# Neighbourhood attention on one core: the first steps reordered, V projected in six matmuls, and the low shift of V in two transfers

## The chip, the cores and the metric

The kernel runs on one core of a Trainium2 chip. The metric is the device time of one execution in microseconds (us); lower is better. The engines are TensorE (PE; its weight loads are shown apart as PEld), VectorE (DVE), ScalarE (ACT), GpSimd (POOL) and SyncE (SP), which here only issues transfers.

## The reference

Each pixel of a 224 x 224 image with 192 channels attends to 7 x 7 neighbours that lie two pixels apart, clipped at the border. Everything is bf16.

```python
H = W = 224; C = 192; ks, dil = 7, 2; half = 6
qkv = x @ wqkv
q, k, v = (qkv[..., :C], qkv[..., C:2*C], qkv[..., 2*C:])
r0 = clip(arange(H) - half, 0, H - 1 - 12)      # first of the 7 rows, the same for columns
...                                             # nidx: the 49 neighbours r0 + 0, 2, .. 12
logits = einsum('bnc,bnkc->bnk', q, k[nidx]) * C ** -0.5
p = softmax(logits)
out = einsum('bnk,bnkc->bnc', p, v[nidx]) @ wo
```

## The kernel before

**Algebra.** Neither Q nor K is made. The setup forms A = wq wk^T (scaled; tiles AW) and W' = wv wo (tiles WP). G = x A is made per query tile, the scores are G against x itself, and V' = x W' already holds the output projection. The 192 channels are split into 128 + 64, so each product has two passes: XA holds the 128, XB the other 64. The partitions that XB has left carry marks: one-hot rows and columns and large negative numbers, which mask keys outside a query's window. G carries the matching marks. `g_col` and `g_row` write these, and `marks` the ones in XB.

**Tiling.** Dilation 2 splits the image by the parity of rows and of columns. `rc` is the row parity. The two column parities `cc` sit side by side in most tiles. There are 14 steps `n` (7 row tiles `ti` by 2 row parities), and each has 7 pairs `m` of column blocks. A column block `s` is 16 rows by 8 columns of queries per parity. `k` counts the 98 pairs.

**Stages of a pair.** `stage1`: the scores into `s` (PE), their maximum `nmx` (DVE). `stage1b`: exp into `p` (ACT). `stage2`: transposes of `p` into `pt_ps` (PE), copied to `pt_sb`. `stage3`: `pt_sb` times V into `o_ps` (PE). `stage4`: division by the sum, and the output transfers. Pair k runs stage 1, pair k - 1 stage 2, and pair k - 2 stages 3 and 4 in the same iteration.

**Work for the next step.** It lies between the pairs. `g_items` makes G in four groups of column blocks: two `whole` products (`pg`, evicted to `g`), and one `halves` product (`pgh`, evicted to `gx`, from which POOL copies into `g`, L456). `v_item` makes one of the 14 V blocks: `v_mms` (L336) issues eight matmuls of 192 columns into `pv`, in two halves h of 64 partitions that lie side by side on PE, and the result is evicted to VF (`vf`). V's lhsT is XS (`xs`): `sort_items` copies a band of 16 image rows from XA and from X1 into the order that V needs, three copies for each row parity. A V block needs two neighbouring bands. `xb_items` copies X1 into XB, two copies. `load_items` issues three transposing loads per band on SP's queue. X1 has two buffers.

**The shifted copies of V.** A query half of 8 rows reads 16 key rows. VD (`vd`) holds V with its halves moved: `vd_low` sends VF[64:128] to VD[0:64] and `vd_high` sends VF[0:64] to VD[64:128]. Both are transfers between SBUF tiles, with 14 blocks of 385 columns in all. `vd_low(rc, 0, 7)` stands at pair m = 5 and 7 to 14 at m = 1 of the next step. VF of that parity is written anew, block by block, from the next step's first pair on. Before the first step VD[0][0:64] is filled by two transfers from VF[1] on ACT's queue (L642); these values only meet probabilities that are zero.

**Order.** `in_order` fixes every engine's program order as it is written in the code, so an engine stands still when its next instruction is not ready. POOL's outputs of block 0 (`out_dram<-o_s`, L588) and its sorts go through the list `pool_q`. Each pair takes four items from it with `pool_do(4)`, and new sorts go to its front. Step 0 is special: bands 0 and 1 are copied and sorted by DVE and POOL before the first pair, and `first_sort` and `v_first` make the upper half of step 1's V. In step 0 the evictions are split between ACT and DVE by the place of an item in a list (L702).

Of the kernel before, what the change touches and what calls it, by code (L numbers as in the profile page):

```python
# [8 lines left out]
BF = mybir.dt.bfloat16  # L9
# [89 lines left out]
def kernel(  # L99
# [212 lines left out]
    for which in range(2):  # L312
        for key in ((0, 0), (1, 0), (0, 1), (1, 1)):
# [4 lines left out]
            if which:  # L318
                nc.scalar.copy(out=WP[key][p0:p0 + cn, :], in_=pt[p0:p0 + cn, 0:C])
# [16 lines left out]
    def v_mms(pv, at):  # L336
        for cc in range(2):
            for pas in range(2):
                for h in range(2):
                    k = 1 if pas else 2 * cc  # L340
                    nc.tensor.matmul(pv[64 * h:64 * h + 64, cc * C:(cc + 1) * C], lhsT=at(k, h), rhs=WP[(cc, pas)][:], start=(pas == 0), stop=(pas == 1))  # L341
# [262 lines left out]
    act, dve, pool = nc.scalar.copy, nc.vector.tensor_copy, nc.gpsimd.tensor_copy  # L604
    pool_q = []
# [23 lines left out]
    sort1 = sort_items(1, 0, pool)  # L629
    for it in sort1[2:] + sort1[:2]:  # L630
        it()
# [10 lines left out]
    for (c0, c1) in ((7, 14), (0, 7)):  # L642
        nc.scalar.dma_start(out=VD[0][0:64, c0:c1, 0:VP - 1], in_=VF[1][0:64, 7:14, 0:VP - 1])
# [3 lines left out]
    for k in range(NP + 2):  # L647
# [3 lines left out]
        if J:  # L651
# [5 lines left out]
            if n == 0:  # L657
                w128 = (v0[:9] + gw0[2:4], v0[9:] + gw0[4:6], gw0[6:8] + vs[0:3], gw[0:2] + vs[3:6], gw[2:4] + vs[6:9], gw[4:6] + vs[9:12], gw[6:8] + vs[12:])[m]
# [6 lines left out]
            if k == 0:  # L665
                marks(1, MM, 2 * MM, dve)
# [21 lines left out]
        first = n == 0 and k >= 2  # L688
        if k >= 2 and not first:
            stage4(pairs[k - 2], 1)  # L690
# [11 lines left out]
        for i, it in enumerate(w128):  # L702
            it(n == 0 and (i in (0, 3 if m == 2 else 4) if first else i % 2 == 1))
            if n == 0 and it is v0[6]:
                vd_high(0, 13, 14)
                vd_high(0, 0, 6)
            if n == 0 and it is v0[13]:
                vd_high(0, 6, 13)
            if first and i == 0:
                stage4(pairs[k - 2], 1)  # L710
            if k == 1 and i == 1:
                xb2.pop(0)()
            if it is vs[6]:
                vd_high(rc1, 0, 7, nc.scalar if n == 0 else nc.sync)
            if it is vs[13]:
                vd_high(rc1, 7, 14, nc.scalar if n == 0 else nc.sync)
        if n == 0 and m == 0:
            xb2.pop(0)()
# [64 lines left out]
```

## Time and profile before

| | us |
|---|---|
| median of 3 runs | 361.81 (361.01 to 361.90) |
| the profiled execution | 360.78 |
| its span | 359.0 |
| PE busy / PEld busy | 332.3 / 306.7 |
| DVE / ACT / POOL busy | 314.3 / 308.5 / 283.0 |
| granted TensorE clock, mean | 0.996 |

The profile shows one execution. Its span runs from the first instruction of the program to the last. The profiled execution took 1.78 us more than its span. Rows of a timeline read: start, duration, engine, line, operation, output tile <- input tiles, shape, count, and in brackets how long the engine had been idle and what ended that. Rows of a window read: length, then busy time and number of instructions of each engine, the granted clock, the share of the DMA engines and GB/s. A wait row gives total, number and longest.

### The profile page before, as it was taken

The numbers are of one execution on the slowest core, as the hardware profiler recorded it, in microseconds if no ns is written. First come the engines' busy times: TensorE is split into PE (matmuls) and PEld (weight loads), VectorE is DVE, ScalarE is ACT, GpSimd is POOL, SyncE is SP. The second block draws the span as 40 slices with busy tenths as digits, with TensorE's granted clock in tenths as the row PEclk, the third lists the DMA queues.
The fourth block names the chain that finished last, engine by engine and source line by source line (L and its number), as shares of the span: only waits on it lengthen the run. The fifth ranks groups of instructions, "written<-read, shape, count | busy, mean of one in ns | idle before, by whom it ended". The sixth has DMA issues, their size and how long they took to land.

```text
span 359.0 us, 19453 instructions
## 1 busy us (share of the span) xinstructions
PE 332.3 (93%) x8120; PEld 306.7 (85%) x8120; DVE 314.3 (88%) x741; ACT 308.5 (86%) x824; POOL 283.0 (79%) x448
## 2 busy tenths in 40 slices
PE   4778997998999999999999999999999999999872
PEld 2666876997999999999989998899999999999762
DVE  8977996997998989889989999799998989989893
ACT  6456776997999999999999998999999989999893
POOL 8976899999896987969869699596995878374182
PEclk9999999999999999999999999999999999999998
DMA  9999986899988989789898998988989855645424
GB/s 188 214 187 171 184 178 163 173 176 189 154 199 193 191 175 176 177 200 201 167 179 188 179 199 187 188 184 181 194 185 188 182 139 125 138 101 116 107 67 91
DMA packets 137539, 60.79 MB, mean 169 GB/s; under 512 B 88578, under 2 KB 136927, under 8 KB 137452
## 3 DMA queue, kind: packets, MB, share of 16 engines
q1 hardware_dynamic: 129124, 55.63, 78.0%
q10 hardware_dynamic: 3048, 2.23, 3.3%
q0 software_dynamic: 5280, 1.71, 2.9%
q8 instruction: 63, 1.03, 1.2%
q14 instruction: 24, 0.20, 0.2%
HBM read 0.29 MB, written 19.27 MB: 54 GB/s over the span
## 4 chain that ended last, share of the span: by engine, by line
PE 71%; POOL 12%; DVE 9%; ACT 4%; issue 2%; DMA 2%; DVEq 0%; ACTq 0%; POOLq 0%
PE s L497 15%; PE pv L341 15%; PE o_ps L536 15%; PE pg L421 10%; PE pt_ps L526 10%; PE pgh L421 5%; POOL out_dram L588 3%; POOL xs L170 3%; ACT p L507 2%; POOL g L456 2%; POOL xb L160 2%; DMA vd<-vf 2%; DVE xb L160 1%; DVE nmx L499 1%; POOL out_dram L565 1%
## 5 line engine op out<-in xcount | busy, mean ns | idle before, releaser
L507 ACT ACTIVATE p<-s,nmx 128x224 bf16<-128x224 f32 x392 | 149.7, 449 | 25.0 <-DVE nmx L499 21.5
L499 DVE TENSOR_REDUCE nmx<-s 128x2 f32<-128x392 f32 (+1 forms) x196 | 102.6, 564 | 19.8 <-PE s L497 18.4
L456 POOL COPY g<-gx 64x512 bf16<-64x512 bf16 (+1 forms) x110 | 62.1, 564 | 52.7 <-ACT gx L331 47.3
L341 PE MATMUL pv<-wp,xs 128*64 128x192 bf16 x1624 | 92.3, 249 | 11.7 <-DVE xs L366 3.6
L341 PEld LDWEIGHTS <-xs 128*64 128x64 bf16 x1624 | 78.7, 111 | 24.3 <-issue 7.6
L559 DVE TENSOR_TENSOR o_sb<-o_ps,rs 128x384 bf16<-128x384 f32 x169 | 94.2, 557 | 5.9
L331 ACT CAST vf<-pv 128x384 bf16<-128x384 f32 x193 | 87.3, 519 | 11.5 <-PE pv L341 9.4
L588 POOL DMA_DIRECT2D out_dram<-o_s x150 | 84.3, 569 | 9.0 <-DVE rs L542 7.8
L497 PE MATMUL s<-xa,g 128*64 128x196 bf16 (+6 forms) x990 | 82.8, 233 | 1.6 <-DVE g L329 0.8
L536 PE MATMUL o_ps<-vd,pt_sb 128*64 128x193 bf16 x784 | 81.8, 246 | 2.4 <-ACT pt_sb L527 2.1
L497 PE MATMUL s<-xb,g 128*64 128x196 bf16 (+7 forms) x990 | 82.3, 232 | 0.6 <-DVE g L329 0.4
L536 PE MATMUL o_ps<-vf,pt_sb 128*64 128x193 bf16 x784 | 81.8, 246 | 0.0
L497 PEld LDWEIGHTS <-g 128*64 128x64 bf16 x1980 | 78.2, 110 | 4.1 <-issue 2.0
L536 PEld LDWEIGHTS <-pt_sb 128*64 128x64 bf16 x1568 | 71.6, 109 | 4.0 <-ACT pt_sb L527 3.2
L527 DVE COPY pt_sb<-pt_ps 128x1024 bf16<-128x1024 bf16 x92 | 63.1, 686 | 5.9 <-PE pt_ps L526 0.8
L526 PE MATMUL pt_ps<-ident,p 128*64 128x128 bf16 x1552 | 63.9, 219 | 0.0
L526 PEld LDWEIGHTS <-p 128*64 128x64 bf16 x1552 | 57.3, 110 | 4.7
L331 ACT CAST g<-pg 128x512 bf16<-128x512 f32 (+4 forms) x136 | 57.5, 468 | 2.4 <-PE pg L421 2.2
L421 PEld LDWEIGHTS <-aw 128*64 128x64 bf16 x1320 | 55.5, 110 | 3.9 <-issue 0.6
L421 PE MATMUL pg<-xb,aw 128*64 128x512 bf16 (+9 forms) x440 | 54.5, 269 | 0.2 <-DVE xb L160 0.2
L421 PE MATMUL pg<-xa,aw 128*64 128x512 bf16 (+9 forms) x440 | 52.8, 270 | 0.1
L170 POOL COPY xs<-xa 128x896 bf16<-128x896 bf16 x52 | 47.4, 939 | 1.4
(73 smaller groups left out, 281.3 us busy)
## 6 DMA issues: line engine op xcount, KB each, us to landing
vd<-vf SPq DMA_DIRECT2D x47, 336.9 KB
out_dram<-o_sb SPq DMA_DIRECT2D x156, 96.0 KB
vd<-vf ACTq DMA_DIRECT2D x4, 336.9 KB
out_dram<-o_s POOLq DMA_DIRECT2D x78, 9.0 KB, 3.7
out_dram<-o_sb SPq DMA_DIRECT2D x13, 78.0 KB
out_dram<-xs SPq DMA_DIRECT2D x13, 78.0 KB
vd<-vf SPq DMA_DIRECT2D x2, 337.8 KB
xa<-in_x_dram SPq DMA_TRANSPOSE x28
```

Source lines behind the costliest of these rows:

```text
L331: nc.scalar.copy(out=out_, in_=in_)
L341: nc.tensor.matmul(pv[64 * h:64 * h + 64, cc * C:(cc + 1) * C], lhsT=at(k, h), rhs=WP[(cc, pas)][:], start=(pas == 0), stop=(pas == 1))
L421: nc.tensor.matmul(o, lhsT=l, rhs=r, start=(pas == 0), stop=(pas == 1))
L456: nc.gpsimd.tensor_copy(out=G[rc][cc][p:p + 64, 1, s0:s0 + ns, :], in_=gx[p:p + 64, 0:ns * 128].rearrange("p (s q) -> p s q", q=128))
L497: nc.tensor.matmul(o, lhsT=w, rhs=r, start=(pas == 0), stop=(pas == 1))
L499: nc.vector.tensor_reduce(out=nmx[:], in_=_win(s_ps, 0, 128, lo, [[256, 2], [16, 14], [1, 16 - lo]]), axis=AX.XY, op=ALU.max, negate=True)
L507: nc.scalar.activation(out=J.p[:, ab, cc, :, z:z + 112].rearrange("p q (r k) -> p q r k", k=8), in_=_win(s_ps, 0, 128, cc * 256, [[8, 2], ...
L526: nc.tensor.transpose(pt_ps[64 * h:64 * h + 64, 4 * ab + 2 * cc + q, :], J.p[:, ab, cc, q, 64 * h:64 * h + 64], ident[:])
L527: (nc.scalar.copy if J.n == NSTEP - 1 and J.m < 5 else nc.vector.tensor_copy)(out=J.pt[:], in_=pt_ps[:])
L536: nc.tensor.matmul(o_ps[64 * h:64 * h + 64, cc * 193:cc * 193 + 193], lhsT=J.pt[:, 4 * ab + 2 * cc + q, 64 * h:64 * h + 64], rhs=V[h][:, ( ...
L559: nc.vector.tensor_tensor(out=o_sb[:], in0=_win(o_ps, 0, 128, 0, [[194, 2], [1, C]]), in1=rs[:].unsqueeze(2).to_broadcast([128, 2, C]), op ...
L588: pool_q.append(lambda dst=dst, p=p, m=n * nj, cc=cc: nc.gpsimd.dma_start(out=dst.rearrange("j i c -> i j c"), in_=o_sb[p:p + m, cc, :]))
```

## The change

1. **V in six matmuls.** The two 64-row passes of W' now lie side by side in one tile WB. `v_mms` issues two matmuls of 384 columns (the 64 leftover channels, for both column parities) and then four of 192, which add to the same accumulators. All 203 V blocks are made so.
2. **The fill of VD[0][0:64]** is one ACT copy of a broadcast column (64 partitions x 14 x 385) after the last W' eviction, and the two transfers on ACT's queue are gone.
3. **Band 1's sort for parity 0** is split: DVE does two of its three copies and the marks of XB[1] (before: in the first pair) ahead of the first V. POOL does the third, and `g_col` for blocks 4 to 13 only after it (before: ahead of all three).
4. **Band 3's** XB copies and sort come at pair 4 of step 0 (before: 5), **band 4's** at pair 3 of step 1 (before: 4).
5. **`vd_low` of blocks 0 to 6** becomes two transfers: 0 to 3 at pair 4 and 4 to 6 at pair 5. This holds for steps 1 to 11, so eleven transfers are added.
6. Step 0's items stand in a written plan, PLAN. Order and engine of each are those that the lists gave before.

```diff
+    WB = pers.tile([128, 2, C], BF, name="wb")
...
-        WP[key] = pers.tile([128, C], BF, name="wp%d%d" % key)
+        WP[key] = pers.tile([128, C], BF, name="wp%d%d" % key)[:] if cn == 128 else WB[:, key[0], :]
...
+    nc.scalar.copy(out=VD[0][0:64, :, 0:VP - 1], in_=E[0:64, 0:1].unsqueeze(2).to_broadcast([64, NSLOT, VP - 1]))
     setup_cm.__exit__(None, None, None)
...
     def v_mms(pv, at):
+        for h in range(2):
+            nc.tensor.matmul(pv[64 * h:64 * h + 64, 0:2 * C], lhsT=at(1, h), rhs=WB[:].rearrange("p t c -> p (t c)"), start=True, stop=False, skip_group_check=True)
         for cc in range(2):
-            for pas in range(2):
-                for h in range(2):
-                    k = 1 if pas else 2 * cc
-                    nc.tensor.matmul(pv[64 * h:64 * h + 64, cc * C:(cc + 1) * C], lhsT=at(k, h), rhs=WP[(cc, pas)][:], start=(pas == 0), stop=(pas == 1))
+            for h in range(2):
+                nc.tensor.matmul(pv[64 * h:64 * h + 64, cc * C:(cc + 1) * C], lhsT=at(2 * cc, h), rhs=WP[(cc, 0)], start=False, stop=True, skip_group_check=True)
...
-    g_col(0, 0, 4, 10, pool)
     for it in load_items(2):
         it()
     for it in first_sort(dve) + xb_items(0, dve) + xb_items(1, dve) + sort_items(0, 0, dve):
         it()
+    srt = sort_items(1, 0, dve)
+    srt[2]()
+    srt[0]()
+    marks(1, MM, 2 * MM, dve)
+    sort_items(1, 0, pool)[1]()
+    g_col(0, 0, 4, 10, pool)
     for j in range(7):
         v_first(j)(False)
...
-    sort1 = sort_items(1, 0, pool)
-    for it in sort1[2:] + sort1[:2]:
-        it()
...
-    for (c0, c1) in ((7, 14), (0, 7)):
-        nc.scalar.dma_start(out=VD[0][0:64, c0:c1, 0:VP - 1], in_=VF[1][0:64, 7:14, 0:VP - 1])
...
-            if k == 0:
-                marks(1, MM, 2 * MM, dve)
...
-        if 0 < n and m == 5 and n + 2 < NSTEP:
-            vd_low(J.rc, 0, 7)
+        if 0 < n and m in (4, 5) and n + 2 < NSTEP:
+            vd_low(J.rc, *((0, 4) if m == 4 else (4, 7)))
...
-            add = {0: sort_items(1, 1, pool), 1: sort_items(2, 1, pool), 3: sort_items(2, 0, pool), 5: xb_items(3, pool) + sort_items(3, 0, pool)}.get(m, [])
+            add = {0: sort_items(1, 1, pool), 1: sort_items(2, 1, pool), 3: sort_items(2, 0, pool), 4: xb_items(3, pool) + sort_items(3, 0, pool)}.get(m, [])
...
-            if m in (2, 4) and n + 3 < NBAND:
+            if m in ((2, 4) if n > 1 else (3,)) and n + 3 < NBAND:
                 srt = sort_items(n + 3, J.rc, pool)
                 one, two = xb_items(n + 3, pool) + srt[2:], srt[:2]
-                add = (two if m == 4 else one) if n > 1 else one + two if m == 4 else []
+                add = (two if m == 4 else one) if n > 1 else one + two
```

More of the change, by code (lines that the diff above doesn't have):

```diff
@@ L604 @@
     act, dve, pool = nc.scalar.copy, nc.vector.tensor_copy, nc.gpsimd.tensor_copy
+    PLAN = (
+        "Va:0 Vd:1 Va:2 Vd:3 Va:4 Vd:5 Va:6 R-:13:14 R-:0:6 Vd:7 Va:8 Gd:2 Ga:3 X-",
+        "Va:9 Vd:10 X- Va:11 Vd:12 Va:13 R-:6:13 Gd:4 Ga:5",
+        "Gd:6 N- Ga:7 Wa:0 Wd:1 Wa:2",
+        "Hd:0 N- Ha:1 Wa:3 Wa:4 Wd:5",
+        "Hd:2 N- Ha:3 Wa:6 Ta:0:7 Wa:7 Wd:8",
+        "Hd:4 N- Ha:5 Wa:9 Wa:10 Wd:11",
+        "Hd:6 N- Ha:7 Wa:12 Wa:13 Ta:7:14",
+    )
     pool_q = []
@@ L657 @@
             if n == 0:
-                w128 = (v0[:9] + gw0[2:4], v0[9:] + gw0[4:6], gw0[6:8] + vs[0:3], gw[0:2] + vs[3:6], gw[2:4] + vs[6:9], gw[4:6] + vs[9:12], gw[6:8] + vs[12:])[m]
                 w64 = (gh0 + gh)[m + 1:m + 2]
@@ L686 @@
             stage2(pairs[k - 1])
-        first = n == 0 and k >= 2
-        if k >= 2 and not first:
+        if k >= 2 and n > 0:
             stage4(pairs[k - 2], 1)
```

26 lines of the change are left out of this document (14 added, 12 removed).

## The prediction

> **What bounds it now.** I read the page, then the stretches, the waits, and the timelines of PE, VectorE (DVE), POOL and ScalarE (ACT) where PE stands still.
>
> ```profile
> span 359.0 us, 19453 instructions
> PE 332.3 (93%) x8120; PEld 306.7 (85%) x8120; DVE 314.3 (88%) x741; ACT 308.5 (86%) x824; POOL 283.0 (79%) x448
> GB/s 188 214 187 171 184 178 163 173 176 189 154 199 193 191 175 176 177 200 201 167 179 188 179 199 187 188 184 181 194 185 188 182 139 125 138 101 116 107 67 91
> 80.00:90.00 10.00, 8.57 (x212) 7.71 (x208) 7.26 (x19) 7.61 (x23) 9.66 (x14) 1.00 0.84 172
> 160.00:200.00 40.00, 39.96 (x1060) 38.24 (x1056) 36.77 (x89) 37.82 (x103) 35.57 (x51) 1.00 0.92 184
> ```
>
> In a stretch row PE, PEld, DVE, ACT and POOL follow the length. From 160 to 200 us PE is busy all but 0.04 us and ACT rests 2.18 us in 40. There only PE's own work counts. Around 80 to 90 POOL is the fullest engine and PE stands still for 1.4 us. Those stops are the first place to gain:
>
> ```profile
> PE pv L341 <- POOL xs L170: 3.6, 3, 2.3
> ACT vf L331 <- DMA vd<-vf: 1.3, 1, 1.3
> 60.31 0.69 PE L341 MATMUL pv<-wp,xs 128*64 128x192 bf16 x12 [2.34 <-POOL xs L170]
> 83.93 0.36 PE L341 MATMUL pv<-wp,xs 128*64 128x192 bf16 x4 [0.69 <-POOL xs L170]
> 84.80 0.44 PE L341 MATMUL pv<-wp,xs 128*64 128x192 bf16 x6 [0.52 <-POOL xs L170]
> 225.06 0.52 PE L341 MATMUL pv<-wp,xs 128*64 128x192 bf16 x8 [1.08 <-ACT g L331]
> ```
>
> PE waits 2.34 us for POOL's sort of band 3, 0.69 + 0.52 us for band 4, and 1.08 us behind an ACT that had waited 1.3 us for a low shift still reading the buffer it was to overwrite. Since PE is full afterwards, what goes from these stops goes from the end.
>
> **Part 1, before the first pair.** The chain here is DVE's.
>
> ```profile
> 11.61 5.24 DVE L160 COPY xb<-x 64x1792 bf16<-64x1792 bf16 x4
> 16.88 2.04 DVE L170 COPY xs<-xa 128x896 bf16<-128x896 bf16 x2
> 18.84 0.42 DVE L170 COPY xs<-x 128x896 bf16<-128x896 bf16 x1
> 19.19 0.60 DVE L329 CAST g<-pg 128x24 bf16<-128x24 f32 x4
> 20.80 1.07 DVE L499 TENSOR_REDUCE nmx<-s 128x2 f32<-128x420 f32 x2 [0.35 <-PE s L497]
> 21.79 1.07 DVE L233 COPY xb<-xb 64x3584 bf16<-64x3584 bf16 x1
> 28.47 0.62 DVE L160 COPY xb<-x 64x1792 bf16<-64x1792 bf16 x1 [0.68 <-DMA x<-in_x_dram]
> 11.98 3.12 POOL L256 COPY g<-ch 32x1280 bf16<-32x1280 bf16 x2
> 15.16 1.20 POOL L170 COPY xs<-x 128x896 bf16<-128x896 bf16 x1
> 16.32 2.36 POOL L170 COPY xs<-xa 128x896 bf16<-128x896 bf16 x2
> ```
>
> The same xb copy takes 0.62 us at 28.47, with POOL idle, and 5.24 / 4 = 1.31 us while POOL copies; xs takes 0.42 against 2.04 / 2 = 1.02. Starts and ends interleave: each engine waits for the other's copy to end. After the change POOL's next copy is the last sort of band 1, which needs that band's last load. Six loads of 128 x 1792 x 2 B, 2.75 MB, at the 188 to 214 GB/s of the first two slices from about 2 us on give 16 us (the old row bounds it: the second copy at 16.32 had begun by 17.7). Until then POOL rests, and DVE runs alone: from 11.61, four xb at 0.62, five xs at 0.42 (two are new) and the marks at 1.07 are 5.65 us, ending at 17.3. Before, it got to its first eviction at 19.19, with the marks still to come at 21.79. PE's product is ready by about then:
>
> ```profile
> 7.89 0.31 ACT L319 CAST wp<-prA 64x192 bf16<-64x192 f32 x1
> 12.47 0.48 ACT L331 CAST vf<-pv 128x384 bf16<-128x384 f32 x1 [4.27 <-PE pv L341]
> 17.38 0.56 ACT L331 CAST g<-pg 128x24 bf16<-128x24 f32 x4 [1.25 <-PE pg L421]
> L331 ACT CAST gx<-pgh 128x128 bf16<-128x128 f32 x25 | 5.5, 274 | 0.4 <-PE pgh L421 0.2
> L527 ACT COPY pt_sb<-pt_ps 128x1024 bf16<-128x1024 bf16 x5 | 5.1, 1018 | 0.1
> ```
>
> ACT evicts the first product at 17.38, so DVE's start moves from 19.19 to about 17.4: 1.8 us. The marks' 1.07 us no longer stand behind the first maximum, but ACT follows that maximum, so I add none (bound above 2.5). Below: if the last load comes a little later than DVE or earlier, POOL's three copies (0.93 as later rows have it, twice 3.12 / 2 = 1.56) come between DVE's last ones. DVE then reaches the eviction 0.6 us late and gets back the marks: 0.3 us. I take 1.8: DVE's last sort ends at 16.2, its marks need only start before the load has landed, and the 16 us counts bytes alone. If the load is first by a little, POOL's one sort goes ahead and the gain is about 0.9, between the two.
>
> The new ACT copy has 14 x 385 = 5390 elements. Between the last two rows an element costs (1018 - 274) / 896 = 0.83 ns, so 4.6 us; by 1018 / 1024 it is 5.4. It starts at 8.20 and ends at 12.8 to 13.6, in an idle time of 4.27 us that ended at 12.47. The seven evictions behind it, 0.48 us each, then end by 16.2 to 17.0, still ahead of 17.4: nothing. Without that cover it would cost its 4.6 us. It waits for nothing but POOL's fills of that buffer, which stand ahead of all POOL copies above. The two transfers it replaces, 2 x 64 x 7 x 770 B = 0.69 MB, free 3.5 us of the DMA queues at 0.2 MB/us; DVE's 0.68 us wait at 28.47 should go, but PE's scores were not ready earlier: nothing (to +0.6, within the bound above).
>
> **Part 2, bands 3 and 4.**
>
> ```profile
> 48.09 2.30 POOL L588 DMA_DIRECT2D out_dram<-o_s  x4
> 52.27 3.39 POOL L160 COPY xb<-x 64x1792 bf16<-64x1792 bf16 x2
> 55.72 1.80 POOL L170 COPY xs<-xa 128x896 bf16<-128x896 bf16 x2
> 59.32 0.93 POOL L170 COPY xs<-x 128x896 bf16<-128x896 bf16 x1
> 72.74 4.52 POOL L588 DMA_DIRECT2D out_dram<-o_s  x8
> 78.62 3.39 POOL L160 COPY xb<-x 64x1792 bf16<-64x1792 bf16 x2
> 82.95 1.80 POOL L170 COPY xs<-xa 128x896 bf16<-128x896 bf16 x2
> ```
>
> Each pair lets POOL take four queued items. Band 3's five copies now start where the four output transfers stood: 48.09 + 3.39 + 1.80 = 53.3, then 1.8 us for the next pair's own POOL work (the gap 57.5 to 59.32), then 0.93: done at 56.1 instead of 60.25. PE wanted it at 60.31 - 2.34 = 57.97, so that stop goes, with 1.9 us to spare. The copies for the next step that follow come 3.39 + 1.80 - 2.30 = 2.9 us later, and the four output transfers a pair later; what reads those copies is in the next step.
>
> Band 4's copies now start after the first four of the eight transfers at 72.74: 75.0 + 3.39 + two sorts 1.8 + the next pair's copies 1.3 + 0.9 = 82.4, not 84.75. But POOL has no idle time here and gets no faster from PE's 2.34 us. PE would arrive 2.34 us earlier and wait about 1.5 us, more than now. Across both places the end comes at 82.4 instead of 84.8: **2.3 us** in all, not 3.55. Bounds: 3.55 if POOL keeps up, 1.0 if the moved work makes a later copy late.
>
> **Part 3, the low shift.** Blocks 0 to 3 leave one pair earlier and are smaller, and ACT overwrites block 0 first; the 1.08 us stop at 225 goes. It occurs once in thirteen steps, so it is a near miss that other executions may not have: **1.1**, bounds 0 and 1.3. Eleven more transfers are issued, one per step; their price is below. In SyncE's queue the new one stands behind the output transfers of the pair that reads the blocks last, so its wait has ended when its turn comes and holds nothing up.
>
> **Part 4, six matmuls per V block instead of eight** (also in the diff).
>
> ```profile
> 285.06 0.61 PE L526 MATMUL pt_ps<-ident,p 128*64 128x128 bf16 x15
> 285.45 0.40 PE L421 MATMUL pg<-xa,aw 128*64 128x416 bf16 x2
> 285.64 0.40 PE L421 MATMUL pg<-xb,aw 128*64 128x416 bf16 x2
> 285.97 0.82 PE L341 MATMUL pv<-wp,xs 128*64 128x192 bf16 x15
> 286.58 0.21 PE L497 MATMUL s<-xa,g 128*64 128x98 bf16 x1
> ```
>
> From start to start one matmul takes 0.39 / 15 = 26 ns at 128 columns, 0.61 / 15 = 41 at 192 and 0.19 / 2 = 95 at 416: 0.20, 0.21 and 0.23 ns a column. Two matmuls of 384 columns replace four of 192: 2 x 81 to 88 ns against 164. Over the 154 blocks made while PE is full (11 steps x 14) that is -0.3 to +1.8 us. I take **0**: the new rhs is read contiguously, as in the 128 and 192 rows, and the 416 one in 13 pieces.
>
> **Sum.** 1.8 + 2.3 + 1.1 + 0 = 5.2 us. The profiled execution took 360.78 us (its span 359.0 and 1.78 around it), so 355.6; the median of the runs is 361.81, 1.03 above it, so **356.6 us**.
>
> **Rivals.**
> *The start gives nothing* (0.2): POOL's copies fall between DVE's last three, as above. For it: the load's 16 us and DVE's 16.2 for its last sort lie close. Part 1 gives 0.3: 358.1 us. The Trainium skill (SBUF — State Buffer, "SBUF: two separate sides") says that whichever of the two starts first keeps the shared port for the whole instruction; the 1.31 against 0.62 us agree.
>
> *Everything comes* (0.12): POOL keeps up, the marks' time counts: 2.5 + 3.55 + 1.3 = 7.35, so 354.5 us.
>
> *The weight loader is PE's pace* (0.03): the page's 306.7 us for 8120 loads are 38 ns each; two fewer in 154 blocks are 11.6 us, just within ACT's rest of 2.18 in 40 us: 345 us. Against it: 26 ns at 128 columns is below 38. The Trainium skill (TensorE: Matmul & The Clock Gate, "Back-to-back issue gap") gives about 81 ns at 128 columns and 131 at 512 for a stream of load and matmul; interpolated to 89 at 192 and 114 at 384, that is an estimate of 129 ns saved per block, or 10 us with two matmuls side by side. The trace does not agree: 26 and 41 ns.
>
> *SyncE's queue becomes the pace, slower* (0.06):
>
> ```profile
> 216.89 0.62 SPq L352 DMA_DIRECT2D vd<-vf  x1
> SPq L565 <- DVE o_sb L559: 54.5, 70, 2.4
> ```
>
> Each extra issue takes 0.62 us, 11 x 0.62 = 6.8 us, ahead of output and input transfers in the same queue. It decides once the queue has under 0.62 us of rest per step. Then part 3 is lost and 6.8 - 4.1 = 2.7 us come on top: 364.5 us. Against it: the queue waits 54.5 us on one producer alone, 4 us per step. The Trainium skill (DMA: Bandwidth & Descriptors, "Rules for kernel authors") says to coalesce small transfers into large ones. Its fixed 2.0 us per transfer (same page, "Anatomy of one DMA") would make an estimate of 22 us; no run so far shows that price.
>
> *The stops only move* (0.07): ACT, with 2.18 us of rest in 40, is the true pace, and each stop that PE loses comes back as a wait for an eviction, so only about 0.3 us is left: 361.5 us. Against it: from 80 to 90 ACT is busy 7.61 of 10.
>
> **Chances.** The forecast has 0.52. A measurement of this kernel tells 0.3%, 1.1 us, from no change. Faster: forecast, start, everything, weight loader, 0.87; same 0.07; slower 0.06. The range 354.0 to 360.0 holds the forecast, the start and everything (0.84), with part 4's cost of up to 1.8 on the forecast; the weight loader's 345, SyncE's 364.5 and the stops' 361.5 lie outside.
>
> **What would show it.** Right: the first nmx near 19 us; no POOL wait near 58; a wait of about 1.5 us near 79; no DMA wait of ACT; POOL idle from 12 to 16. Wrong: xb copies still at 1.3 us, the ACT copy over 6 us, pv over 0.35 us a block, or output transfers of SyncE that no longer wait for DVE.

## The result and the profile after

| | before | after |
|---|---|---|
| median of the runs, us | 361.47 (359.65 to 368.30, 21 runs) | 358.71 (356.64 to 362.73, 21 runs) |
| ratio | | 0.9936, 95% interval 0.991 to 0.9961 |
| profiled execution, us | 360.78 | 360.73 |

The changed kernel is 0.64% faster: 2.3 us, between 1.4 and 3.3, where 5.2 were forecast. (Medians are of all runs; ratios and stage times leave disturbed ones out.) The profiled execution of it lies 2.0 us above its median and shows nothing of the gain at its end. So the trace was read by stages: for each pair the start of its first nmx, after against before. These differences are -0.77 us at pair 0, -0.44 at pair 1, -2.50 at pair 8, -2.78 at pair 15, then -1.35 at pair 28, -0.89 at pair 42, +1.38 at pair 56, +0.22 at pair 58 and 0 at the end. Something was gained by 83 us and lost again between 100 and 215 us.

The page of the changed kernel, its span and its busy times:

```profile
span 359.0 us, 18669 instructions
PE 333.0 (93%) x7714; PEld 302.1 (84%) x7714; DVE 312.5 (87%) x743; ACT 312.1 (87%) x825; POOL 280.2 (78%) x446
```

The stretches of the changed kernel (length, then PE, PEld, DVE, ACT, POOL, clock, DMA share, GB/s):

```profile
80.00:90.00 10.00, 8.97 (x196) 7.90 (x193) 8.07 (x20) 8.41 (x26) 9.64 (x16) 1.00 0.92 165
160.00:200.00 40.00, 39.29 (x980) 36.60 (x976) 35.67 (x86) 36.46 (x100) 34.55 (x49) 1.00 0.95 183
```

Around 80 PE now stands for 1.03 us instead of 1.43. But from 160 to 200, where it stood for 0.04, it stands for 0.71. The waits of the changed kernel say for what (total, number, longest):

```profile
PE pv L340 <- DVE xs L368: 4.0, 1, 4.0
PE pv L340 <- ACT gx L333: 3.0, 4, 1.5
DVE o_sb L561 <- DMA out_dram<-o_sb: 2.3, 2, 1.3
PE o_ps L538 <- DMA vd<-vf: 2.1, 3, 1.1
PE pv L343 <- POOL xs L170: 1.0, 1, 1.0
ACT vf L333 <- DMA vd<-vf: 0.7, 2, 0.4
```

The 4.0 us are the wait for the first sorted copy at the start (3.6 before). Of POOL's sorts (3.6 us before) 1.0 is left. In its place PE waits three times for a shifted copy of V, a wait that the list of before does not have. It also waits 3.0 us behind evictions of ACT (0.4 for `gx` before); 1.48 us of them stand at 30.48, 0.32 at 58.05 and 0.64 at 212.48, shortly after ACT itself had stood for 1.82 us (210.78). The timeline of PE in the changed kernel shows where:

```profile
58.05 0.35 PE L340 MATMUL pv<-wb,xs 128*64 128x384 bf16 x2 [0.32 <-ACT gx L333]
82.11 0.27 PE L343 MATMUL pv<-wp,xs 128*64 128x192 bf16 x1 [0.99 <-POOL xs L170]
110.55 0.24 PE L538 MATMUL o_ps<-vd,pt_sb 128*64 128x193 bf16 x1 [1.13 <-DMA vd<-vf]
179.97 0.24 PE L538 MATMUL o_ps<-vd,pt_sb 128*64 128x193 bf16 x1 [0.66 <-DMA vd<-vf]
285.94 0.36 PE L340 MATMUL pv<-wb,xs 128*64 128x384 bf16 x2
286.11 0.36 PE L343 MATMUL pv<-wp,xs 128*64 128x192 bf16 x4
286.27 0.36 PE L340 MATMUL pv<-wb,xs 128*64 128x384 bf16 x2
```

The stop near 58 is down from 2.34 to 0.32 us, the one for band 4 is 0.99 at 82.11, and no stop stands near 225. In the full stage two matmuls of 384 columns take 0.17 us from start to start, as four of 192 do (285.94, 286.11, 286.27).

DVE in the changed kernel, at the start:

```profile
11.61 2.72 DVE L160 COPY xb<-x 64x1792 bf16<-64x1792 bf16 x4
15.87 1.08 DVE L233 COPY xb<-xb 64x3584 bf16<-64x3584 bf16 x1
18.40 0.62 DVE L331 CAST g<-pg 128x24 bf16<-128x24 f32 x4 [1.45 <-PE pg L423]
20.03 1.07 DVE L501 TENSOR_REDUCE nmx<-s 128x2 f32<-128x420 f32 x2 [0.35 <-PE s L499]
26.21 2.43 DVE L160 COPY xb<-x 64x1792 bf16<-64x1792 bf16 x1
28.57 1.05 DVE L501 TENSOR_REDUCE nmx<-s 128x2 f32<-128x420 f32 x2
```

POOL and ACT in the changed kernel:

```profile
16.23 1.51 POOL L170 COPY xs<-xa 128x896 bf16<-128x896 bf16 x1 [4.31 <-DMA xa<-in_x_dram]
25.48 1.80 POOL L170 COPY xs<-xa 128x896 bf16<-128x896 bf16 x2
27.23 0.93 POOL L170 COPY xs<-x 128x896 bf16<-128x896 bf16 x1
54.74 0.93 POOL L170 COPY xs<-x 128x896 bf16<-128x896 bf16 x1
8.23 4.68 ACT L323 COPY vd<-e 64x5390 bf16<-64x5390 bf16 x1
17.95 0.56 ACT L333 CAST g<-pg 128x24 bf16<-128x24 f32 x4 [0.96 <-PE pg L423]
```

DVE's copies run nearly as forecast: 0.68 us each (0.62 forecast) beside an idle POOL, marks done at 16.95. Then DVE waits 1.45 us for PE. And at 26.21 the XB copy of band 2, whose load now lands before DVE asks for it, runs into POOL's three sorts (25.48 to 28.16). It takes 2.43 us, where it took 0.62 before, and the second nmx stands right behind it: 28.57 against 29.01. POOL for its part works without a rest from 16.23, when band 1's load has landed, to 28.16.

### The profile page after: what moved, and what is told of

Same layout as the page of the kernel before. It is cut to its first block, busy times and chain, and to the rows that moved or that the text cites. A ratio compares the mean times of both kernels' runs of the same rounds, so it can differ in the third digit from the quotient of the medians.

```text
span 359.0 us, 18669 instructions
## 1 busy us (share of the span) xinstructions
PE 333.0 (93%) x7714; PEld 302.1 (84%) x7714; DVE 312.5 (87%) x743; ACT 312.1 (87%) x825; POOL 280.2 (78%) x446
## 4 chain that ended last, share of the span: by engine, by line
PE 67%; ACT 9%; DVE 9%; POOL 5%; DMA 5%; issue 3%; DVEq 0%; ACTq 0%; SPq 0%; POOLq 0%
PE s L499 14%; PE o_ps L538 14%; PE pg L423 9%; PE pt_ps L528 9%; PE pv L340 8%; PE pv L343 7%; ACT p L509 6%; PE pgh L423 5%; DMA vd<-vf 4%; DVE nmx L501 2%; POOL xs L170 2%; ACT gx L333 1%; POOL out_dram L590 1%; DMA out_dram<-o_sb 1%; POOL xb L160 1%
## 5 line engine op out<-in xcount | busy, mean ns | idle before, releaser
L501 DVE TENSOR_REDUCE nmx<-s 128x2 f32<-128x392 f32 (+1 forms) x196 | 102.5, 564 | 16.2 <-PE s L499 15.0
L333 ACT CAST vf<-pv 128x384 bf16<-128x384 f32 x193 | 88.8, 526 | 8.5 <-PE pv L343 3.0
L499 PE MATMUL s<-xa,g 128*64 128x196 bf16 (+7 forms) x990 | 82.1, 233 | 1.2 <-ACT p L509 0.3
L340 PE MATMUL pv<-wb,xs 128*64 128x384 bf16 x406 | 72.7, 334 | 9.0 <-DVE xs L368 4.0
L343 PE MATMUL pv<-wp,xs 128*64 128x192 bf16 x812 | 73.2, 250 | 1.0 <-POOL xs L170 1.0
L343 PEld LDWEIGHTS <-xs 128*64 128x64 bf16 x812 | 60.1, 112 | 9.6 <-POOL xs L170 1.2
L423 PEld LDWEIGHTS <-aw 128*64 128x64 bf16 x1320 | 54.6, 110 | 3.2
```

The source lines that it names most:

```text
L333: nc.scalar.copy(out=out_, in_=in_)
L340: nc.tensor.matmul(pv[64 * h:64 * h + 64, 0:2 * C], lhsT=at(1, h), rhs=WB[:].rearrange("p t c -> p (t c)"), start=True, stop=False, skip_g ...
L423: nc.tensor.matmul(o, lhsT=l, rhs=r, start=(pas == 0), stop=(pas == 1))
L499: nc.tensor.matmul(o, lhsT=w, rhs=r, start=(pas == 0), stop=(pas == 1))
L501: nc.vector.tensor_reduce(out=nmx[:], in_=_win(s_ps, 0, 128, lo, [[256, 2], [16, 14], [1, 16 - lo]]), axis=AX.XY, op=ALU.max, negate=True)
```

## The experiments

Three questions were open. Why did part 1 bring 0.45 us instead of 1.8? What makes V's shifted copies late: the number of issues in SyncE's queue, or the transfer engines that carry them? And does each part do alone what it does in the whole? Medians are compared as ratios to the kernel before. The stages come from one profiled execution of each kernel, here for those that the argument needs:

| kernel, times in us | first nmx | second nmx | pair 15 | pairs 15 to 56 | pairs 56 to 93 |
|---|---|---|---|---|---|
| before | 20.80 | 29.01 | 85.98 | 132.43 | 120.01 |
| before, part 1 alone | 19.63 | 28.56 | 85.48 | 132.43 | 119.76 |
| before, part 3 alone | 20.81 | 29.13 | 86.05 | 132.47 | 120.03 |
| before, part 4 alone | 20.81 | 29.29 | 86.60 | 132.68 | 118.66 |
| after | 20.03 | 28.57 | 83.20 | 136.58 | 118.59 |
| after, a second profile | 19.89 | 28.56 | 83.17 | 137.92 | 118.56 |
| after, one low transfer | 19.32 | 28.55 | 84.73 | 135.54 | 119.45 |
| after, low shift in four | 19.87 | 28.67 | 83.30 | 142.11 | 124.25 |
| after, low shift on ACT's queue | 19.57 | 28.56 | 86.91 | 132.27 | 118.56 |
| the same from step 2 on | 19.99 | 28.56 | 83.19 | 134.21 | 119.31 |
| after, on POOL's queue from step 2 on | 20.56 | 28.57 | 84.80 | 132.89 | 118.57 |
| after, band 2's copy late | 19.83 | 27.02 | 81.88 | 134.22 | 118.59 |
| the same, second profile | 19.01 | 26.19 | 81.06 | 133.13 | 118.58 |
| the same, POOL's queue | 20.36 | 27.55 | 82.39 | 132.57 | 118.58 |

Four of these profiles hold a stretch of 3.41 us in which the granted clock was half: part 1 alone from 60.4 us on, one low transfer from 32.4, low shift on ACT's queue from 80.7 and low shift in four from 234.9. The last section says what it costs.

### The changed kernel again, and its parts alone

The changed kernel without an edit:

> The changed kernel once more, beside the others of this group, with a second profile. Theory A (SyncE's queue: its rest per step fell from about 3.2 us to 1.7 us with the eleven added transfers, so late shifts of V stop PE): the PE stops on vd between 100 and 215 us, 2.1 us in the first profile, come again in some of the steps, and SyncE rests under 2 us per step. Theory B (chance: such stops hit either kernel anywhere): they may be missing altogether, with SyncE's rest still under 2 us. Time: 2 to 3 us under the kernel before by both.

Measured: 359.99 us, ratio 0.9942 (0.9906 to 0.9979). The gains at the front come again to 0.03 us (second nmx 28.56, pair 15 at 83.17). The loss from pair 15 to 56 is 5.5 us this time against 4.15: it is of the kernel, but its size changes from execution to execution.

Part 1 alone: the ACT copy in place of the two fill transfers, and the following lines, in place of those that the change takes out:

```diff
+    srt = sort_items(1, 0, dve)
+    srt[2]()
+    srt[0]()
+    marks(1, MM, 2 * MM, dve)
+    sort_items(1, 0, pool)[1]()
     g_col(0, 0, 4, 10, pool)
```

> The kernel before with part 1 alone: the fill of VD by ACT, band 1's sort split between DVE and POOL ahead of the first V, the marks ahead of the first pair. V stays in eight matmuls, so the first V block starts with the copies that are sorted first. If the matmul order of part 4 is what held the first V back, then the first nmx comes at 18.9 to 19.3 us, against 20.80 before and 20.03 with all parts. If it is the XS copies' own times or the weight loads, it comes at about 20.0 here too. In either case the gain at the second pair is below 1 us, for the XB copy of band 2 meets POOL's sorts here as well; at the end 0 to 1 us are left, 360.5 to 361.5.

Measured: 361.11 us, ratio 1.0007 (0.9977 to 1.0037). The first nmx came at 19.63, the second at 28.56, to 0.01 us where the whole change has it. Two rows tell the rest, the first of DVE, the second of PE, in this kernel:

```profile
25.82 2.82 DVE L160 COPY xb<-x 64x1792 bf16<-64x1792 bf16 x1
59.85 0.84 PE L342 MATMUL pv<-wp,xs 128*64 128x192 bf16 x13 [2.34 <-POOL xs L170]
```

The copy ends with POOL's sorts here too, and near 60 PE waits for POOL's sort of band 3 as before. At pair 8 this kernel is 0.02 us ahead of the one before: what the start gives, POOL takes back 30 us later.

Part 2 alone (the edits to bands 3 and 4 of the diff):

> The kernel before with only bands 3 and 4 one pair earlier. The prediction's part 2: PE's stop of 2.34 us near 58 goes and one of about 1.5 us stays near 81: 2.3 us less at the start of step 2. Theory A: SyncE's rest shrinks from then on and 1 to 2 us of it are lost by step 8, so 0.5 to 1.5 us are left at the end; theory B: all 2.3 us are left on the average.

Measured: 360.55 us, ratio 0.9994 (0.9964 to 1.0024). By the interval at most 1.3 us of the 2.3 reach the end when the part stands alone. Where the rest goes is not shown.

Part 3 alone (the two transfers of the diff):

> The kernel before with only the low shift split. Prediction's part 3: 1.1 us faster than the kernel before (0 to 1.3). Theory A: SyncE's rest falls from about 3.2 to 1.7 us per step and PE stops on vd appear: 0 to 2 us slower than the kernel before.

Measured: 361.56 us, ratio 1.0003 (0.9971 to 1.0036). Behind a later PE eleven more issues cost nothing (132.47 against 132.43). The stop at 224 is gone, but 1.3 us are lost at pair 61, near 234.

Part 4 alone (the new `v_mms`, with WB):

> The kernel before with part 4 alone, V in six matmuls instead of eight, the 384-column pair first. Forecast of the prediction: 0, bounds -0.3 to +1.8 us of cost over 154 blocks. [...] If the last-sorted copy, which now goes first, holds blocks back in step 0, 0.3 to 0.9 us more. If the weight loads set PE's pace, over 5 us less.

Measured: 360.85 us, ratio 0.9989 (0.9961 to 1.0017): nothing, as forecast. This kernel has the low shift in one transfer, and pairs 56 to 93 take 118.66: here the stop at 224 is absent without any split, as it is with part 1 alone.

### What makes V's copies late

The low shift in one transfer again, at pair 5, in the changed kernel:

```diff
-        if 0 < n and m in (4, 5) and n + 2 < NSTEP:
-            vd_low(J.rc, *((0, 4) if m == 4 else (4, 7)))
+        if 0 < n and m == 5 and n + 2 < NSTEP:
+            vd_low(J.rc, 0, 7)
```

> The changed kernel with the low shift of blocks 0 to 6 as one transfer at pair 5 again. Theory A: SyncE's rest per step goes back to about 3 us, the stops of PE on vd go, ACT may stop once for about 1 us as in the kernel before: 0 to 2 us faster than the changed kernel. Theory B and the prediction's part 3: about 1.1 us slower than the changed kernel, by ACT's stops on the low shift.

Measured: 360.23 us, ratio 0.9971 (0.9946 to 0.9995). Pairs 15 to 56 still lose 3.1 us, now through ACT, which waits 3.7 us there for transfers to have read VF. (Its later pair 15 comes in part from the half clock at 32.4.) So the split is not the cause of the loss. Its own worth, 0.9971 against 0.9936 and 0.9942, is about 1 us inside the changed kernel, and the intervals overlap: it is not shown.

The other way, four transfers with the same bytes (blocks 0-1, 2-3 at pair 4, 4-5, 6 at pair 5), 22 more issues:

> The changed kernel with the low shift of blocks 0 to 6 in four transfers (2, 2, 2 and 1 blocks) instead of two: same bytes, 22 more issues on SyncE's queue, 1.24 us per step. Theory A: SyncE's rest of 1.7 us per step is used up and PE, ACT or DVE stop more in steps 2 to 10: 2 to 8 us slower than the changed kernel. Theory B (stops by chance): within 1 us of it.

Measured: 372.12 us, ratio 1.0327 (1.0277 to 1.0377): 13.4 us over the changed kernel, 0.61 us for each added issue. That this meets the 0.62 us of one issue so closely is partly chance: four executions were measured, and the profiled one has the stretch at half clock.

Both parts issued from ACT's queue:

```diff
-            vd_low(J.rc, *((0, 4) if m == 4 else (4, 7)))
+            vd_low(J.rc, *((0, 4) if m == 4 else (4, 7)), nc.scalar)
```

> The changed kernel with the two parts of the low shift (blocks 0 to 3 and 4 to 6) issued on ACT's queue instead of SyncE's, in steps 1 to 11. The bytes and the number of transfers stay. Theory A: SyncE's rest rises to 3.5 us or more per step and the stops on vd go: 1 to 2 us faster than the changed kernel, less what 22 issues of 0.6 us cost on ACT where they are not hidden. If instead the transfer engines' throughput is the limit (theory C), the stops on vd stay: same time or slower.

Measured: 362.02 us, ratio 0.9985 (0.995 to 1.0021). All of the loss stands in step 1, at pair 14; ACT's row there:

```profile
78.88 0.58 ACT L333 CAST g<-pg 128x512 bf16<-128x512 f32 x1 [4.62 <-DMA xa<-in_x_dram]
```

The issue stands in ACT's own order, and what ACT has to do behind it waits 4.62 us. The stretch at half clock follows, from 80.7 on. From pair 15 on nothing is lost: 132.27. Hence the same from step 2 on, with step 1 left on SyncE's queue, and then POOL's queue in ACT's place:

> The changed kernel with the two parts of the low shift issued on ACT's queue in steps 2 to 11 and on SyncE's in step 1. With all of them on ACT, one 4.6 us stop of ACT stood in step 1, before an issue that waited for an earlier load, and no stop on vd stood in steps 2 to 10. Theory A (SyncE's queue is the pace in steps 2 to 8): without that stop the gain of 2.4 to 2.8 us that stands at the start of step 2 stays to the end: 356 to 358 us in the profile, 0.990 to 0.993 of the kernel before or better. Theory C (the transfer engines' throughput): the gain shrinks over steps 2 to 8 as it does in the changed kernel.

> The same two parts issued on POOL's queue in steps 2 to 11. Theory A: the stops on vd and on outputs go as on ACT's queue, and POOL, which has about 4 us of rest per step from step 3 on, pays 0.6 us or more per issue: 0.990 to 0.994. Theory C: no gain over the changed kernel. Against both: POOL is full in step 2, where its sorts would come late and stop PE by about 1 us.

Measured: 359.74 us, ratio 0.9967 (0.9935 to 1.0), and 358.69 us, ratio 0.9936 (0.9906 to 0.9965). The stretch from 100 to 200 us of the kernel before, of the changed kernel, of the one with four transfers and of the one on POOL's queue, one row each:

```profile
100.00:200.00 100.00, 99.92 (x2579) 94.94 (x2575) 91.22 (x219) 93.98 (x255) 84.00 (x119) 1.00 0.93 186
```

```profile
100.00:200.00 100.00, 97.79 (x2394) 91.09 (x2390) 88.38 (x211) 90.72 (x247) 82.53 (x118) 1.00 0.93 182
```

```profile
100.00:200.00 100.00, 94.94 (x2305) 88.80 (x2303) 86.20 (x205) 88.41 (x238) 78.58 (x110) 1.00 0.84 175
```

```profile
100.00:200.00 100.00, 99.91 (x2460) 93.82 (x2457) 91.30 (x219) 93.97 (x255) 89.39 (x128) 1.00 0.89 187
```

PE stands for 0.08, 2.21, 5.06 and 0.09 us of the 100. With four transfers the transfer engines are emptier (share 0.84 and 175 GB/s against 0.93 and 182) and PE waits longer. With the same transfers on another queue they move more (187) and PE does not wait. So it is not the engines, but SyncE's order.

Between 86 and 264 us SyncE has 155 issues before and 163 after. An issue that waits for nothing begins 0.05 to 0.1 us after the end of the one before, so only a later start is rest. Before the change 31 issues begin over 0.11 us after the one before, with 14.7 us between them in sum. In the changed kernel it is 4 issues and 1.1 us, or 0.14 us per step of 22.4. Two rows of before, then five of the changed kernel:

```profile
102.67 0.62 SPq L352 DMA_DIRECT2D vd<-vf  x1
103.68 1.10 SPq L565 DMA_DIRECT2D out_dram<-o_sb  x1
```

```profile
101.19 0.62 SPq L354 DMA_DIRECT2D vd<-vf  x1
101.90 1.21 SPq L567 DMA_DIRECT2D out_dram<-o_sb  x2
103.21 0.62 SPq L354 DMA_DIRECT2D vd<-vf  x1
103.92 1.23 SPq L567 DMA_DIRECT2D out_dram<-o_sb  x2
105.24 1.79 SPq L357 DMA_DIRECT2D vd<-vf  x1
```

Before, 0.39 us lie free ahead of 103.68; after, each row begins 0.1 us or less behind the last.

The same rest is 24.9 us (41 issues) with the issues on POOL's queue, and 2.4 us (8 of 154) in the kernel with one low transfer: there the queue is full without any added issue. The time in the issues themselves rises from 149.9 us before to 161.6 after and 162.7 with one low transfer. Eight added issues explain 5.0 of the 11.7 us after; why issues of the same kinds take longer is open, and so whether SyncE is held by the issuing itself or by transfers that still stand in its queue.

Counted over pairs 15 to 56 alone, the kernels of the table with under 2 us of rest lose 1.8 to 9.7 us there against the one before. Those with 7.5 us or more stay within 0.5 us of it, but for one: with the issues on ACT's queue from step 2 on, ACT again waits behind an issue, 2.13 us at 100.69. The second profile of the late copy lies between, with 5.1 us of rest and 0.7 us lost.

But the end says that the move is no gain: the kernel on POOL's queue has the ratio of the changed kernel. Its profile reaches pair 15 later (84.80 against 83.20), but up to there the two programs are the same, so this is chance: DVE waits 2.6 us for a free output tile and PE 1.82 us behind ACT. From pair 15 on it keeps what the changed kernel loses. Why its median is then no lower is open.

### What holds the start back

Two edits to the changed kernel: the four matmuls of 192 columns first in `v_mms`, the pair of 384, whose sorted copy comes last, at the end; and the XB copy of band 2 one pair later:

```diff
-        "Va:0 Vd:1 Va:2 Vd:3 Va:4 Vd:5 Va:6 R-:13:14 R-:0:6 Vd:7 Va:8 Gd:2 Ga:3 X-",
-        "Va:9 Vd:10 X- Va:11 Vd:12 Va:13 R-:6:13 Gd:4 Ga:5",
+        "Va:0 Vd:1 Va:2 Vd:3 Va:4 Vd:5 Va:6 R-:13:14 R-:0:6 Vd:7 Va:8 Gd:2 Ga:3",
+        "Va:9 Vd:10 X- Va:11 Vd:12 X- Va:13 R-:6:13 Gd:4 Ga:5",
```

> The changed kernel with two edits to its start: in v_mms the four 192-column matmuls go first and the 384-column pair, which needs the copy XS that is sorted last, goes last; and the XB copy of band 2 moves from pair 0 to pair 1. Theory of part 1: the forecast 1.8 us shrank to 0.45 because the first V blocks now wait for the last of the sorted copies, and because DVE's XB copy of band 2 ran against three POOL copies (2.43 us instead of 0.62). Then the first nmx comes at about 19.1 us (20.03 in the changed kernel, 20.80 before), and by the second pair the kernel is 1.5 to 2.0 us ahead of the one before (0.44 in the changed kernel). Rival on part 1: PE's slow pace of the first blocks (0.64 us each) comes from something else, not from the order; then the first nmx stays at 20.0 and only the collision's part, up to 1.8 us, comes at the second pair or not at all. On the end: if SyncE's queue is the pace of steps 2 to 8, whatever is gained here is given back, and the time stays within 0.4 us of the changed kernel's (358.7); if PE is the pace throughout, 357.0 to 357.5.

Measured: 356.88 us, ratio 0.9872 (0.9835 to 0.9909). First nmx 19.88, second 27.06. The queue did not take the gain back: the theory said 358.7 +/- 0.4. In this kernel, and in the next, the start flag stands on the first matmuls of both column parities, and V does not hold the full product; the instructions are the same in number and shape as in the later kernels, which set the flag on the first parity's alone.

With the low shift on POOL's queue from step 2 on as well:

> The kernel of the front edits, with both parts of the low shift issued from POOL's queue from step 2 on and from SyncE's in step 1. The bytes and the number of transfers are those of the changed kernel. If the issues on SyncE's queue are what gives the gain back, then what the front edits gain lasts: 1.0 to 1.7 us below the same kernel without the front edits (358.7 there), 357.0 to 357.7, a ratio to the kernel before of about 0.989 to 0.991, and no stop of PE for vd after 90 us of over 0.3 us. If the transfer engines themselves are the limit, it comes out at 358.5 to 359, as the changed kernel does.

Measured: 356.37 us, ratio 0.9848 (0.9816 to 0.988).

Then each edit alone. The order of the matmuls:

```diff
-        for h in range(2):
-            nc.tensor.matmul(pv[64 * h:64 * h + 64, 0:2 * C], lhsT=at(1, h), rhs=WB[:].rearrange("p t c -> p (t c)"), start=True, stop=False, ...)
...
-                nc.tensor.matmul(pv[...], lhsT=at(2 * cc, h), rhs=WP[(cc, 0)], start=False, stop=True, ...)
+                nc.tensor.matmul(pv[...], lhsT=at(2 * cc, h), rhs=WP[(cc, 0)], start=(cc == 0), stop=False, ...)
+        for h in range(2):
+            nc.tensor.matmul(pv[64 * h:64 * h + 64, 0:2 * C], lhsT=at(1, h), rhs=WB[:].rearrange("p t c -> p (t c)"), start=False, stop=True, ...)
```

> The changed kernel with the order of the six matmuls turned in all V blocks: the four of 192 columns first, the pair of 384 last. The accumulators of both column parities are started by the first matmul alone. If the two front edits act through the second pair's nmx, this one alone does little: the first nmx comes 0 to 0.8 us earlier (19.2 to 20.0), by the moment at which PE's half pace ends, the second stays 0.45 us ahead of the kernel before, and the time is that of the changed kernel, 358.3 to 359.1. Rival: the order counts in every step (the weights of the 192-column matmuls load under the 384-column pair or not), then the end is 1 to 2 us below the changed kernel's without an earlier second pair.

Measured: 359.20 us, ratio 0.9938 (0.9912 to 0.9963): nothing. The first nmx came at 19.30, the second at 28.56 all the same. And the copy of band 2 alone:

> The changed kernel with the XB copy of band 2 at pair 1 instead of pair 0, nothing else. If the collision of DVE's copy with POOL's three sorts is what kept part 1 at 0.45 us, the second nmx comes 1.3 to 2.0 us ahead of the kernel before, though the first does not come earlier than 20.0. At the end: 357.0 to 357.6 if the gain lasts; 358.3 to 359.1 if SyncE's queue takes it back.

Measured: 356.01 us, ratio 0.9849 (0.9832 to 0.9867): all of it. DVE in this kernel:

```profile
19.83 1.07 DVE L501 TENSOR_REDUCE nmx<-s 128x2 f32<-128x420 f32 x2 [0.35 <-PE s L499]
27.02 1.07 DVE L501 TENSOR_REDUCE nmx<-s 128x2 f32<-128x420 f32 x2 [0.92 <-PE s L499]
29.32 0.73 DVE L160 COPY xb<-x 64x1792 bf16<-64x1792 bf16 x1
```

The copy takes 0.73 us at 29.32, behind POOL's sorts, and the second nmx waits for PE alone. With the start changed and the copy in its old place the second nmx came between 28.55 and 28.57 in eight profiles of nine (28.67 in the ninth), whether the first stood at 19.30 or at 20.56; with the copy late it follows the first by 7.17 to 7.19 us in seven profiles. The old place was a wall at the end of POOL's sorts, 28.16 us, that nothing tried ahead of it moved.

Both edits, accumulators started once, and the same on POOL's queue:

> Both front edits, with the accumulators of both column parities started by the first matmul alone; instructions and order are those of the first kernel with both edits. The same time, 356.4 to 357.4, a ratio to the kernel before of 0.984 to 0.991. If that gain came from the matmul order and the copy in equal parts, the two single edits give half each; if from the copy alone, the copy alone gives all of it.

> Both front edits and the low shift on POOL's queue from step 2 on, the accumulators started once. As the same kernel before it, 355.9 to 357.0. If the issues on SyncE's queue still cost when the start is earlier, 0.5 to 1.5 us below the kernel with the front edits alone; if not, the same within 0.4 us.

Measured: 357.24 us, ratio 0.9901 (0.9865 to 0.9937), and 356.70 us, ratio 0.9877 (0.9858 to 0.9897). The order of the matmuls adds nothing to the copy. Last, the late copy with SyncE's queue and with POOL's, side by side:

> The changed kernel with the XB copy of band 2 at pair 1, as before, beside the next kernel. Again 355.7 to 356.5 us, a ratio of 0.983 to 0.988; the second nmx 1.3 to 2.0 us ahead of the kernel before, and the stops for vd in steps 2 to 8 between nothing and 2.5 us in sum.

> The same, with the low shift on POOL's queue from step 2 on. Theory: a SyncE queue with 1 to 2 us of rest per step makes vd late in some executions and not in others, by up to 4 us; taking 22 issues from it removes these stops, so its executions lie closer together and the median is 0.3 to 1.0 us lower, 355.0 to 355.9, with no stop for vd after step 2. Rival: the stops came from the start's lateness alone, and with the later copy the queue costs nothing; then both kernels agree within 0.3 us, and POOL's extra issues may even cost 0.2 to 0.5 us.

Measured: 355.94 us (355.13 to 358.73), ratio 0.9869 (0.9825 to 0.9914), and 357.08 us (355.97 to 357.66), ratio 0.9872 (0.984 to 0.9905). POOL's queue again takes the stops away (pairs 15 to 56 in 132.57 us), its six executions lie closer together, and again the median gains nothing. So the best version found is the changed kernel with band 2's XB copy one pair later, 356.0 us, about 5 us below the kernel before.

## Why the prediction was partly wrong

The sign, the parts 2 and 4 and the range held; the size did not. That the range held is partly luck: it was drawn for a start that gives little, not for a gain of part 2 that is lost again behind pair 15.

**Part 1 (1.8 us, measured 0.45).** The copies, the ACT fill (4.68 us for 4.6) and POOL's rest to 16.2 came as written. "PE's product is ready by about then" did not hold in the profiled execution: PE ran at half pace until 16.8 us instead of 14.6 (the last section), so that ACT evicts G at 17.95, not 17.38, and DVE starts at 18.40, not at 17.4. That is chance: where the half pace ended at 14.66, the first nmx came at 19.01, as forecast. The first V block starts at 11.74 instead of 10.84, since it now begins with the copy sorted last, but this costs under 0.1 us: with the half pace ending at 14.67 and 14.66 the seven blocks were through by 15.39 with the four of 192 columns first and by 15.47 with the pair of 384 first. The step that failed was another: "DVE's 0.68 us wait at 28.47 should go, but PE's scores were not ready earlier: nothing". The load that lands earlier lets DVE start its copy 2.3 us earlier, among POOL's sorts, and the copy grows by 1.8 us. Moving only that copy brought the second nmx to 27.02 and 26.19, 2.0 and 2.8 us ahead of before. The prediction had the price of that collision in its own rows, 1.31 against 0.62, and did not carry it to the next place where the two engines meet.

**Part 2 (2.3 us, measured 2.3).** From pair 1 to pair 15 the difference grows from 0.44 to 2.78. Three of four profiles of the same program up to there show these 2.3 us; the fourth shows 0.7 and has the two waits that were named with POOL's queue. Band 3's copies were done at 55.67 (forecast 56.1). The stop for band 4 became 0.99 us, not 1.5, and so the end there comes at 82.11, not 82.4. Alone the part shows no such gain at the end; why is open.

**Part 3 (1.1 us, a size not settled).** The stop at 224 is gone, but it goes in the kernels with part 1 alone and with six matmuls alone too, and moves in the one with the split alone. It was the near miss that the prediction called it.

**Part 4 (0, measured 0).** 0.17 us for two matmuls of 384 columns and for four of 192. The rival in which the weight loader is PE's pace is out: PEld fell from 306.7 to 302.1 us and the pairs kept their time.

**SyncE's queue (0.06, and this is where the rest went).** The rival named the mechanism and the price: 0.62 us an issue, and 0.61 was found for the 22 of the kernel with four transfers. The argument against it was the step that failed: "the queue waits 54.5 us on one producer alone, 4 us per step". That total spreads over the whole span, and it is not rest. The view counts from the end of the last issue to the latest signal of the engine that is waited for, also when that signal comes while the next issue is already running. Between 86 and 264 us it adds up to some 75 us of waits before, 74 after and 72 with four transfers, whether the queue is full or not. Rest between the issues was 1.9 us per step before the change and 0.14 after. So the rival's own condition, under 0.62 us, was met. Its price was not: the 364.5 us were not reached, and by the medians the changed kernel stays 2.8 us ahead. The sign that was to tell the rival, outputs that no longer wait for DVE, is none; SyncE's waits in the changed kernel:

```profile
SPq L567 <- DVE o_sb L561: 45.7, 60, 2.4
```

In profiled executions pairs 15 to 56 then lose 4.15 and 5.5 us; of the 4.15, PE's waits for vd are 2.1 and one behind ACT at 212.48 is 0.64. The forecast priced part 3's issues at nothing while parts 1 and 2 let PE run 2.8 us earlier against the same queue. Taking the split out again did not help (0.9971, with 2.4 us of rest), so it is not the eleven issues alone but the whole order of that queue that then has too little room. The 2.0 us per transfer that the prediction took from the Trainium skill (DMA: Bandwidth & Descriptors, "Anatomy of one DMA — SWDGE (gpsimd) path") stand there for transfers issued by GpSimd; no run here shows that price.

**The sum.** 0.45 + 2.3 + 1.4 (pairs 56 to 93) - 4.15 = 0.0 in the profiled execution; by the medians (2.8 us apart) in a usual execution some 1.4 us are lost there and not 4.15, an estimate. The forecast's 356.6 us is nearly what the late copy reaches, 356.0, but not by the forecast's sum. Of its 2.7 us over the changed kernel 1.5 come at the second pair; why its executions also lose less behind pair 15 (134.22 and 133.13 against 136.58 and 137.92 in pairs 15 to 56) stays open. A part of the gain ahead of pair 15 may also be the stretch at half clock near 32 us, which none of its profiles has (last section); that is not shown.

## What to carry to other kernels

When a load or a copy becomes ready earlier, look at what it will then run beside: an instruction that was hidden by its own lateness can start in the middle of another engine's work, and whatever stands behind it in order will wait for that. Read the rest of an issuing queue in the stage where it is needed, from the starts that come later than the usual gap behind the issue before, and not from a total of its waits over the span. And where a gain disappears, put the stage times of several kernels side by side: a time that stays the same to 0.01 us while what stands before it moves by a microsecond is a wall, and the instruction in front of it is the one to move.

## What the runs showed of the hardware that was not expected

**PE starts at half pace, and the stretch rows print a clock of 1.00 there.** One stretch row of the changed kernel, then the same microsecond in the second profile of the kernel with the late copy:

```profile
15.00:16.00 1.00, 1.00 (x12) 0.71 (x10) 1.00 (x5) 0.68 (x3) 0.00 (x0) 1.00 1.25 249
```

```profile
15.00:16.00 1.00, 1.00 (x32) 0.95 (x30) 1.00 (x5) 1.00 (x4) 0.00 (x0) 1.00 1.18 129
```

In one PE issues 12 matmuls, in the other 32, and both rows print a clock of 1.00. The trace itself has no clock record there: its first record begins at 16.78 us in the one and at 14.66 in the other, at full clock. In the kernels with six matmuls per block the first V blocks go at 0.32 us for two matmuls of 384 columns, and from about that moment on at 0.16. The moment lies between 14.55 us (before) and 17.76 (the first kernel on POOL's queue). In the changed kernel and its variants on POOL's queue or with the late copy the first nmx follows it: 19.01 us where it was 14.66, 19.83 at 16.36, 20.03 at 16.78, 20.56 at 17.76. So up to 1.5 us of the first pair's time are chance, behind a PE that had rested from 7.8 to 10.8 or 11.7. The Trainium skill (TensorE: Matmul & The Clock Gate, "Part 1: The HAM clock gate") says that the array runs at half its clock after a rest and is released by a busy window of some 3.4 us that runs freely; the halved pace agrees, and the 3.4 us fit the later stretches below. The Trainium skill gives the moment a scatter of 0.5 us to either side there; here it moves over 3.1 us among kernels whose PE starts again at 11.74 or 11.75.

Half clock comes back before the program's end in six of the twenty traces, each time for 3.41 us, and there the clock column shows it (0.57 from 32 to 36 us with one low transfer). Each time PE had been busy for only 0.7 to 1.4 us in the 3.41 us before. With one low transfer, the same program as the changed kernel up to there, the stretch from 32.4 us on costs 1.5 us by pair 3. From 29.0 to 32.4 us PE is busy for 1.4 us in the changed kernel's profile, for 2.4 before the change, and for 2.9 and 3.2 in two profiles with the late copy; none of the seven profiles with the late copy has such a stretch. So the wall at 28.16 also brings PE near this loss. How often executions pay it is not shown.

**DVE does not get a turn between POOL's copies.** At 26.21 DVE's copy stood 2.43 us, until POOL's third copy in a row had ended, while these three kept 0.90 to 0.93 us each. At 11.61 before the change the two engines had taken turns. The Trainium skill (SBUF — State Buffer, "SBUF: two separate sides") says that whichever starts first keeps the shared port for its whole instruction; that a wait can reach over several instructions of the other engine is what the trace adds.
